# Weights cast in a software DMA, first loads in pieces and cast on VectorE, and one set of transposes moved by a batch: attention followed by a gated feed-forward, on one core

## The chip, the cores and the metric

The kernel runs on one core of one Trainium2 chip. The metric is the device time of one execution in microseconds (us); lower is better. Medians are over all executions of a kernel; ratios use only those in the fast state. The profile's span is about 1.8 us shorter than the time of the same execution. Two executions in this study (of some 55 of the changed kernels) were far slower than all others; they are shown below, and no ratio uses them.

Names: TensorE is PE, VectorE is DVE, ScalarE is ACT, GpSimd is POOL, SyncE is SP in the profile's lines. PEld is TensorE's weight load. `L203` is line 203 of that kernel's file, so the same operation has different line numbers in different kernels.

## The reference

Eight batches. Grouped attention (16 query heads, 4 key heads, 384 positions, 64 per head), whose output is the input of a feed-forward with a gate that mixes positions:

```python
scores = softmax(q @ k.T / sqrt(D));  x = scores @ v          # per batch and head
h = relu(x @ w_in)                    # 1024 -> 1024
u, v = h[..., :512], h[..., 512:]
v_n = (v - mean(v)) / sqrt(var(v) + 1e-6)
v_s = einsum('ts,bsd->btd', w_spatial, v_n) + b_spatial
out = (u * v_s) @ w_out               # 512 -> 1024
```

All inputs and the output are float32; the kernel computes in float16 with float32 sums.

## The kernel before

TensorE's program order is written by hand. Batch `b`'s attention is nine visits of two score tiles each; into the visits are put the matmuls that sum the values, the transposes of the next batch's k and q, and, from the third visit on, the feed-forward of the batch before (`pv`: the v half of w_in, `pu`: the u half, `psp`: w_spatial, `po`: w_out). So no feed-forward runs during batch 0: there, TensorE has little to do, and until the first `pv` of batch 0's feed-forward (in batch 1's third visit) everything hangs on loads, casts and ScalarE's exp.

The weights are staged: a load on SyncE's queue into one of three float32 buffers, then a cast to float16 on VectorE.

```python
stage = ctx.enter_context(tc.tile_pool(name="stage", bufs=3))
...
def load_w_in(kc):                       # eight of these, four loads each
    st_w = stage.tile([P, DFF], FP32, name=f"st_wi_{kc}", tag="st_w")
    ...
            nc.sync.dma_start(st_w[32 * i : 32 * (i + 1), :], moe_w_in[r0 : r0 + 32, :])
    nc.vector.tensor_copy(w_in16[:, kc, :], st_w)

def load_w_out(m):                       # four of these
    st_w = stage.tile([P, DM], FP32, name=f"st_wo_{m}", tag="st_w")
    nc.sync.dma_start(st_w, moe_w_out[m * P : (m + 1) * P, :])
    nc.vector.tensor_copy(w_out16[:, m, :], st_w)
...
def load_batch(b):
    load_kv(b); load_q(b, 0); load_v(b); load_q(b, 1)      # all on SyncE's queue
    cast_kv(b); cast_q(b, 0); cast_v(b); cast_q(b, 1)      # all on GpSimd
...
load_batch(0)
load_consts()
with tc.manual_schedule(engines={PE}):
    transpose_k(0)
    transpose_q(0, 0, 0); transpose_q(0, 0, 1)
    transpose_q(0, 1, 0); transpose_q(0, 1, 1)             # second group pair, ahead of all scores
    load_bias()
    for kc in range(NKT):
        load_w_in(kc)
    load_ws()                                              # w_spatial
    for m in range(NDT):
        load_w_out(m)
    for b in range(B + 1):
        for vi in range(VISITS if b < B else 1):
            scores(b, [2 * vi, 2 * vi + 1])
            ...
            if vi == 1 and b + 1 < B:
                load_batch(b + 1)
            if b + 1 < B and vi in (4, 5, 6, 7, 8):        # next batch's k, then all its q
                if vi == 4: transpose_k(b + 1)
                else:       transpose_q(b + 1, (vi - 5) // 2, (vi - 5) % 2)
            if b == 0 and vi in (3, 4, 5):
                transpose_ws(vi - 3)
            if vi == 2 and b > 0 or b == B:
                queue += feed_forward(b - 1)
            ...
```

(Lines joined and cut.) The loads of batch 1 come behind all the weights in SyncE's queue, and its first load waits for nothing else.

The softmax here doesn't subtract the row's maximum and nothing guards it: scores larger than these inputs give would overflow.

## Time and profile before

| | before |
|---|---|
| time, median of 3 | 327.24 us |
| profile's span | 324.8 us |
| TensorE busy over the span | 83% |
| first `pv` of batch 0 starts | 65.2 us |
| TensorE busy before that / after that | 26.2 of 65.2 us / 244.2 of 259.6 us |

The table of busy time by stretch, before (columns: stretch in us, then busy us and number of instructions of PE, PEld, DVE, ACT, POOL, then granted TensorE clock, DMA share, GB/s):

```profile
0.00:65.20 65.20, 26.17 (x261) 11.84 (x261) 22.88 (x46) 26.25 (x32) 15.96 (x25) 0.81 0.84 239
65.20:324.80 259.60, 244.20 (x2198) 113.43 (x2196) 139.06 (x270) 159.92 (x218) 23.43 (x29) 0.99 0.26 89
```

From the first `pv` on TensorE is busy 94% of the time, so waits can cost at most 6% there. Before it, TensorE, VectorE, ScalarE and GpSimd are all idle more than half of the time: waits rule. The page's rows of busy tenths, in 40 slices of 8.1 us, before:

```profile
PE   1470118799998999899989998999989998999994
PEclk9996558989999999999999999999999999999999
```

The zero-to-one slices at 24 to 49 us are the hole. What TensorE waited for there, before (who waited for what: us in total, times, longest):

```profile
PE psw_352 L203 <- DVE ws_240 L194: 15.1, 3, 14.6
PE pk_366 L214 <- POOL k_1_281 L111: 6.8, 1, 6.8
PE pk_141 L214 <- POOL k_0_118 L111: 5.0, 1, 5.0
PE pq_1_0_168 L229 <- POOL q_0_1_125 L125: 3.6, 1, 3.6
```

`psw` is a transpose of w_spatial: it waited for VectorE's cast of w_spatial. `pk_366` is the transpose of k_1: it waited for GpSimd's cast of k_1. Neither cast was late for want of an engine: both engines stood idle until the load landed. The chain of waits, before, cut to this stretch (start us, us, what), shows what stood behind them:

```profile
32.15 0.42 SPq L181
32.57 0.04 issue
32.61 0.42 SPq L181
33.03 0.04 issue
33.08 5.17 DMA ws_238<-in_moe_w_spatial_dram
38.24 0.02 issue
38.27 1.80 DVE ws_240 L194 x3
40.07 0.05 issue
40.11 0.30 PE psw_352 L203
```

`SPq L181` is SyncE issuing loads of w_in: w_spatial was loaded only at 33 us, when the last of w_in had found a staging buffer. The same queue makes k_1 later still; GpSimd's timeline, before:

```profile
47.23 0.83 POOL L111 CAST k_1_281<-k_1_273 128x768 f16<-128x768 f32 x1 [33.71 <-DMA k_1_273<-in_k_dram]
```

GpSimd sat idle 33.71 us for a load that was issued behind w_out.

SyncE's queue stopped from 18.0 to 25.75 us in the middle of w_in. VectorE's timeline, before:

```profile
24.10 0.56 DVE L288 TENSOR_TENSOR xt_307<-X_0_0_0_324,rec_0_0_321 128x384 f16<-128x384 f32 x1 [7.87 <-ACT rec_0_0_321 L284]
25.04 0.68 DVE L182 CAST w_in_107<-st_wi_196 128x1024 f16<-128x1024 f32 x1
```

The cast that frees the buffer stands behind batch 0's x (`xt`) in VectorE's order, and VectorE was idle 7.87 us until x could be computed.

### The profile page before, as it was taken

The numbers are of one execution on the slowest core, as the hardware profiler recorded it, in microseconds if no ns is written. First come the engines' busy times: TensorE is split into PE (matmuls) and PEld (weight loads), VectorE is DVE, ScalarE is ACT, GpSimd is POOL, SyncE is SP. The second block draws the span as 40 slices with busy tenths as digits, with TensorE's granted clock in tenths as the row PEclk, the third lists the DMA queues.
The fourth block names the chain that finished last, engine by engine and source line by source line (L and its number), as shares of the span: only waits on it lengthen the run. The fifth ranks groups of instructions, "written<-read, shape, count | busy, mean of one in ns | idle before, by whom it ended". The sixth has DMA issues, their size and how long they took to land.

```text
span 324.8 us, 5856 instructions
## 1 busy us (share of the span) xinstructions
PE 270.4 (83%) x2457; PEld 125.3 (39%) x2457; DVE 161.9 (50%) x316; ACT 186.2 (57%) x249; POOL 39.4 (12%) x54
## 2 busy tenths in 40 slices
PE   1470118799998999899989998999989998999994
PEld 0320003344443544345434543354435443443451
DVE  1604434326653655365645384366546553654574
ACT  1090027946667755857585748576667568675300
POOL 3300015541111111101120112000000000000000
PEclk9996558989999999999999999999999999999999
DMA  7927989994256016601560002100310031003104
GB/s 242 240 68 171 316 262 300 315 302 123 56 196 207 0 50 226 211 1 50 194 218 30 0 23 108 67 0 2 132 65 2 1 131 65 2 0 131 67 0 194
DMA packets 30828, 38.71 MB, mean 119 GB/s; under 512 B 1489, under 2 KB 26066, under 8 KB 30802
## 3 DMA queue, kind: packets, MB, share of 16 engines
q1 hardware_dynamic: 30802, 38.35, 37.0%
q8 instruction: 19, 0.31, 0.4%
q14 instruction: 7, 0.06, 0.1%
HBM read 25.76 MB, written 12.58 MB: 118 GB/s over the span
## 4 chain that ended last, share of the span: by engine, by line
PE 65%; ACT 19%; DMA 7%; SPq 3%; DVE 2%; issue 1%; POOL 1%; DVEq 0%
DMA q_0_1_116<-in_q_dram 3%; DMA q_1_0_275<-in_q_dram 2%; ACT aT_0_262 L257 2%; SPq L181 2%; DMA ws_238<-in_moe_w_spatial_dram 2%; ACT aT_1_3573 L257 1%; ACT aT_1_2647 L257 1%; ACT aT_1_759 L257 1%; ACT aT_1_3119 L257 1%; ACT aT_1_2175 L257 1%; ACT aT_1_1703 L257 1%; ACT aT_1_1231 L257 1%; ACT aT_1_364 L257 1%; PE pv_0_627 L303 1%; ACT aT_0_545 L257 1%
## 5 line engine op out<-in xcount | busy, mean ns | idle before, releaser
L340 PEld LDWEIGHTS <-w_in_107 128*128 128x128 f16 x256 | 24.1, 98 | 18.2 <-issue 2.6
L272 PEld LDWEIGHTS <-ones_103 128*32 128x32 f16 x384 | 7.4, 97 | 15.8 <-issue 14.1
L203 PE MATMUL psw_352<-ident_102,ws_240 128*128 128x128 f16 x3 | 0.9, 287 | 15.1 <-DVE ws_240 L194 15.1
L257 ACT ACTIVATE aT_0_262<-sc_8_357 128x1024 f16<-128x1024 f32 x1 | 1.0, 1024 | 16.9 <-PE sc_8_357 L244 16.9
L257 ACT ACTIVATE aT_0_262<-sc_0_256 128x1024 f16<-128x1024 f32 x1 | 1.0, 1024 | 13.6 <-PE sc_0_256 L244 13.6
L203 PEld LDWEIGHTS <-ws_240 128*128 128x128 f16 x9 | 0.9, 117 | 15.9 <-DVE ws_240 L194 15.9
L214 PE MATMUL pk_366<-ident_102,k_1_281 128*128 128x128 f16 x6 | 0.8, 310 | 6.8 <-POOL k_1_281 L111 6.8
L257 ACT ACTIVATE aT_1_364<-sc_10_380 128x1024 f16<-128x1024 f32 x1 | 1.0, 1024 | 6.9 <-PE sc_10_380 L244 6.9
L214 PE MATMUL pk_141<-ident_102,k_0_118 128*128 128x128 f16 x6 | 0.8, 310 | 5.0 <-POOL k_0_118 L111 5.0
L244 PEld LDWEIGHTS <-kT_148 64*128 64x128 f16 x36 | 1.8, 102 | 8.3 <-issue 7.9
L111 POOL CAST k_1_281<-k_1_273 128x768 f16<-128x768 f32 x1 | 0.8, 829 | 33.7 <-DMA k_1_273<-in_k_dram 33.7
L288 DVE TENSOR_TENSOR xt_307<-X_0_0_0_324,rec_0_0_321 128x384 f16<-128x384 f32 x1 | 0.6, 557 | 7.9 <-ACT rec_0_0_321 L284 7.9
L303 PEld LDWEIGHTS <-xt_307 128*128 128x128 f16 x24 | 2.6, 113 | 4.1 <-issue 2.3
L356 PEld LDWEIGHTS <-bias_ones 128*128 128x128 f16 x32 | 3.1, 98 | 1.9 <-issue 0.7
L229 PE MATMUL pq_1_0_168<-ident_102,q_0_1_125 128*128 128x128 f16 x6 | 0.8, 307 | 3.6 <-POOL q_0_1_125 L125 3.6
L272 PEld LDWEIGHTS <-v_0_123 128*32 128x32 f16 x96 | 2.9, 109 | 2.0 <-issue 1.0
L214 PEld LDWEIGHTS <-k_1_281 128*128 128x128 f16 x6 | 0.6, 137 | 7.7 <-POOL k_1_281 L111 7.7
L379 PEld LDWEIGHTS <-gT_3919 128*128 128x128 f16 x24 | 2.3, 98 | 3.0 <-DVE gT_3919 L365 0.5
L303 PEld LDWEIGHTS <-xt_3511 128*128 128x128 f16 x24 | 2.3, 98 | 2.9 <-issue 0.3
L379 PEld LDWEIGHTS <-gT_2267 128*128 128x128 f16 x24 | 2.2, 97 | 3.0 <-DVE gT_2267 L365 0.6
L379 PEld LDWEIGHTS <-gT_2739 128*128 128x128 f16 x24 | 2.2, 97 | 3.0 <-DVE gT_2739 L365 0.6
L379 PEld LDWEIGHTS <-gT_3211 128*128 128x128 f16 x24 | 2.2, 97 | 3.0 <-DVE gT_3211 L365 0.6
(1178 smaller groups left out, 812.1 us busy)
## 6 DMA issues: line engine op xcount, KB each, us to landing
q_0_0_112<-in_q_dram SPq DMA_DIRECT2D x1, 768.0 KB, 5.6
q_0_1_116<-in_q_dram SPq DMA_DIRECT2D x1, 768.0 KB, 9.4
q_1_0_275<-in_q_dram SPq DMA_DIRECT2D x1, 768.0 KB, 7.6
q_1_1_279<-in_q_dram SPq DMA_DIRECT2D x1, 768.0 KB, 9.5
q_2_0_602<-in_q_dram SPq DMA_DIRECT2D x1, 768.0 KB, 5.5
q_2_1_606<-in_q_dram SPq DMA_DIRECT2D x1, 768.0 KB, 5.5
q_3_0_1074<-in_q_dram SPq DMA_DIRECT2D x1, 768.0 KB, 6.2
q_3_1_1078<-in_q_dram SPq DMA_DIRECT2D x1, 768.0 KB, 6.2
```

The costliest lines, as they stand in the source:

```text
L111: nc.gpsimd.tensor_copy(k16, loaded[("k32", b)].rearrange("p g (t d) -> p t g d", t=NST))
L181: nc.sync.dma_start(st_w[32 * i : 32 * (i + 1), :], moe_w_in[r0 : r0 + 32, :])
L203: nc.tensor.transpose(psw[:, tt, :], ws16[:, tt, st, :], ident16)
L214: nc.tensor.transpose(pk[:, gp, t, :], k16[:, t, 2 * gp : 2 * gp + 2, :].rearrange("p g d -> p (g d)"), ident16,)
L229: nc.tensor.transpose(pq[:, jj, t, :], q16[:, t, 2 * jp + jj, :, :].rearrange("p h d -> p (h d)"), ident16,)
L244: nc.tensor.matmul(sc[:, half, :], kT[b][lo:hi, gp, t, :], rhs[lo:hi, c * 512 : (c + 1) * 512], start=True, stop=True,)
L257: nc.scalar.activation(aT[b, gp][:, t, :, c * 512 : (c + 1) * 512], sc, AF.Exp, scale=scale)
L272: nc.tensor.matmul(dst[32 * i : 32 * (i + 1), 0:S], weights(t, half), a[:, t, half, j * S : (j + 1) * S], start=(t == 0), stop=(t == NST - 1),
L303: nc.tensor.matmul(pv, xt[:, kc, st * P : (st + 1) * P], w_in16[:, kc, DH:DFF], start=(kc == 0), stop=(kc == NKT - 1),)
L340: nc.tensor.matmul(pu[:, 0:S], w_in16[:, kc, mu * P : (mu + 1) * P], xT[b][:, kc, :], start=(kc == 0), stop=(kc == NKT - 1),)
L356: nc.tensor.matmul(psp[:, 0:S], bias_ones, bias_rows, start=True, stop=False)
L379: nc.tensor.matmul(po, gT[:, m, tt * P : (tt + 1) * P], w_out16[:, m, half * 512 : (half + 1) * 512], start=(m == 0), stop=(m == NDT - 1),)
```

## The change

Its intent: no staging of weights, an earlier first score, and transposes only when they are needed. The diff, cut to its core:

```diff
-    stage = ctx.enter_context(tc.tile_pool(name="stage", bufs=3))
+    stage = ctx.enter_context(tc.tile_pool(name="stage", bufs=1))
...
-    def load_w_in(kc):            # 4 loads on nc.sync into st_w, cast by nc.vector
+    def load_w_in(c0, c1):        # 16 casting DMAs for the columns c0:c1
+        for gp in range(2):
+            for half in range(2):
+                for quad in range(2):
+                    ...
+                    for jq in range(2):
+                        i = half * 2 + jq
+                        nc.gpsimd.dma_start(
+                            w_in16[32 * i : 32 * (i + 1), kc : kc + 2, c0:c1], rows[jq]
+                        )
-    def load_w_out(m):            # likewise staged
+    def load_w_out():
+        for h in range(2):
+            nc.gpsimd.dma_start(w_out16[:, 2 * h : 2 * h + 2, :], ...)
...
-    load_batch(0)
     load_consts()
-    with tc.manual_schedule(engines={PE}):
+    with tc.manual_schedule(engines={PE, POOL, SP}):
+        load_k(0)
+        load_q(0, 0, pieces=2)
+        cast_k(0, nc.vector)
+        cast_q(0, 0, nc.vector)
+        load_v(0)
+        load_q(0, 1, pieces=2)
+        cast_v(0, nc.gpsimd)
+        cast_q(0, 1, nc.gpsimd)
+        load_w_in(DH, DFF)        # v half first
+        load_w_in(0, DH)
+        load_w_out()
         transpose_k(0)
         transpose_q(0, 0, 0)
         transpose_q(0, 0, 1)
-        transpose_q(0, 1, 0)
-        transpose_q(0, 1, 1)
...
-                    if vi == 1 and b + 1 < B:
-                        load_batch(b + 1)
-                    if b + 1 < B and vi in (4, 5, 6, 7, 8):
+                    if vi in (1, 2):
+                        transpose_q(b, 1, vi - 1)          # second pair inside its own batch
+                    if vi == 2 and b + 1 < B:
+                        load_batch(b + 1, nc.vector if b == 0 else nc.gpsimd)
+                    if vi >= 6 and b + 1 < B:              # next batch: k and first pair only
...
-                    if b == 0 and vi in (3, 4, 5):
-                        transpose_ws(vi - 3)
+                    if b == 0 and vi == 3:
+                        load_ws()
+                        load_bias()
...
+                    if b == 1:
+                        queue[7:7] = [(0.2, lambda st=st: transpose_ws(st)) for st in range(NST)]
```

`cast_k` and `cast_q` for batch 1 run on VectorE, for later batches on GpSimd; `cast_v` and the second pair's `cast_q` always on GpSimd. A load that changes the type must be issued from GpSimd (the Trainium skill, "DMA: Bandwidth & Descriptors", SWDGE vs HWDGE vs iDMA), so the weights change queue as well as caster.

More of the change, by code (lines that the diff above doesn't have):

```diff
@@ L14 @@
 ALU = mybir.AluOpType
-PE = mybir.EngineType.PE
+PE, POOL, SP = mybir.EngineType.PE, mybir.EngineType.Pool, mybir.EngineType.SP
 @with_exitstack
@@ L89, with load_k @@
     loaded = {}
-    def load_kv(b):
+    def load_k(b):
         k32 = ld.tile([P, HKV, NST * D], FP32, name=f"k32_{b}", tag="k32")
         nc.sync.dma_start(k32, k[b].rearrange("g (p t) d -> p g (t d)", t=NST))
-        loaded[("k32", b)] = k32
+        loaded["k32", b] = k32
     def load_v(b):
@@ L98, in load_v, with load_q, cast_k, cast_v @@
         nc.sync.dma_start(v32, v[b].rearrange("g (p t) d -> p g (t d)", t=NST))
-        loaded[("v32", b)] = v32
-    def load_q(b, gp):
+        loaded["v32", b] = v32
+    def load_q(b, gp, pieces=1):
         q32 = ld.tile([P, 2 * G, NST * D], FP32, name=f"q32_{b}_{gp}", tag=f"q32_{gp}")
-        nc.sync.dma_start(
-            q32,
-            q[b, gp * 2 * G : (gp + 1) * 2 * G].rearrange("h (p t) d -> p h (t d)", t=NST),
-        )
-        loaded[("q32", b, gp)] = q32
-    def cast_kv(b):
-        k16 = qk16.tile([P, NST, HKV, D], FP16, name=f"k16_{b}", tag="k16")
-        nc.gpsimd.tensor_copy(
-            k16, loaded[("k32", b)].rearrange("p g (t d) -> p t g d", t=NST)
-        )
-        loaded[("k16", b)] = k16
-    def cast_v(b):
+        n = 2 * G // pieces
+        for i in range(pieces):
+            h0 = gp * 2 * G + i * n
+            nc.sync.dma_start(
+                q32[:, i * n : (i + 1) * n, :],
+                q[b, h0 : h0 + n].rearrange("h (p t) d -> p h (t d)", t=NST),
+            )
+        loaded["q32", b, gp] = q32
+    def cast_k(b, engine):
+        k16 = qk16.tile([P, NST, HKV, D], FP16, name=f"k16_{b}", tag="k16")
+        engine.tensor_copy(k16, loaded["k32", b].rearrange("p g (t d) -> p t g d", t=NST))
+        loaded["k16", b] = k16
+    def cast_v(b, engine):
         v16 = qk16.tile([P, HKV, NST, D], FP16, name=f"v16_{b}", tag="v16", bufs=3)
-        nc.gpsimd.tensor_copy(v16.rearrange("p g t d -> p g (t d)"), loaded[("v32", b)])
-        loaded[("v16", b)] = v16
-    def cast_q(b, gp):
+        engine.tensor_copy(v16.rearrange("p g t d -> p g (t d)"), loaded["v32", b])
+        loaded["v16", b] = v16
+    def cast_q(b, gp, engine):
         q16 = qk16.tile([P, NST, G, 2, D], FP16, name=f"q16_{b}_{gp}", tag=f"q16_{gp}")
-        q32 = loaded[("q32", b, gp)]
+        q32 = loaded["q32", b, gp]
         for half in range(2):
-            nc.gpsimd.tensor_copy(
+            engine.tensor_copy(
                 q16[:, :, :, half, :],
@@ L128, in cast_q, with load_batch @@
             )
-        loaded[("q16", b, gp)] = q16
-    def load_batch(b):
-        load_kv(b)
+        loaded["q16", b, gp] = q16
+    def load_batch(b, first):
+        load_k(b)
         load_q(b, 0)
+        cast_k(b, first)
+        cast_q(b, 0, first)
         load_v(b)
         load_q(b, 1)
-        cast_kv(b)
-        cast_q(b, 0)
-        cast_v(b)
-        cast_q(b, 1)
+        cast_v(b, nc.gpsimd)
+        cast_q(b, 1, nc.gpsimd)
     ident = cst.tile([P, P], FP32, name="ident")
@@ L171, in load_bias @@
         nc.vector.tensor_copy(lo, lo32)
-    def load_w_in(kc):
-        gp, quad, jj = kc // 4, (kc // 2) % 2, kc % 2
-        st_w = stage.tile([P, DFF], FP32, name=f"st_wi_{kc}", tag="st_w")
-        for half in range(2):
-            for jq in range(2):
-                i = half * 2 + jq
-                head = gp * 2 * G + half * G + quad * 2 + jq
-                r0 = head * D + 32 * jj
-                nc.sync.dma_start(st_w[32 * i : 32 * (i + 1), :], moe_w_in[r0 : r0 + 32, :])
-        nc.vector.tensor_copy(w_in16[:, kc, :], st_w)
-    def load_w_out(m):
-        st_w = stage.tile([P, DM], FP32, name=f"st_wo_{m}", tag="st_w")
-        nc.sync.dma_start(st_w, moe_w_out[m * P : (m + 1) * P, :])
-        nc.vector.tensor_copy(w_out16[:, m, :], st_w)
+    def load_w_in(c0, c1):
+        for gp in range(2):
+            for half in range(2):
+                for quad in range(2):
+                    r0 = (gp * 2 * G + half * G + 2 * quad) * D
+                    rows = moe_w_in[r0 : r0 + 2 * D, c0:c1].rearrange(
+                        "(jq jj r) n -> jq r jj n", jq=2, jj=2
+                    )
+                    kc = gp * 4 + quad * 2
+                    for jq in range(2):
+                        i = half * 2 + jq
+                        nc.gpsimd.dma_start(
+                            w_in16[32 * i : 32 * (i + 1), kc : kc + 2, c0:c1], rows[jq]
+                        )
+    def load_w_out():
+        for h in range(2):
+            nc.gpsimd.dma_start(
+                w_out16[:, 2 * h : 2 * h + 2, :],
+                moe_w_out[2 * h * P : (2 * h + 2) * P, :].rearrange("(m p) n -> p m n", p=P),
+            )
     def load_ws():
@@ L417 @@
         transpose_q(0, 0, 1)
-        transpose_q(0, 1, 0)
-        transpose_q(0, 1, 1)
-        load_bias()
-        for kc in range(NKT):
-            load_w_in(kc)
-        load_ws()
-        for m in range(NDT):
-            load_w_out(m)
         total = sum(t for t, _ in feed_forward(0))
@@ L439 @@
                 if b < B:
-                    if vi == 1 and b + 1 < B:
-                        load_batch(b + 1)
-                    if b + 1 < B and vi in (4, 5, 6, 7, 8):
-                        if vi == 4:
+                    if vi in (1, 2):
+                        transpose_q(b, 1, vi - 1)
+                        done += T_TRANS
+                    if vi == 2 and b + 1 < B:
+                        load_batch(b + 1, nc.vector if b == 0 else nc.gpsimd)
+                    if vi >= 6 and b + 1 < B:
+                        if vi == 6:
                             transpose_k(b + 1)
                         else:
-                            transpose_q(b + 1, (vi - 5) // 2, (vi - 5) % 2)
+                            transpose_q(b + 1, 0, vi - 7)
                         done += T_TRANS
-                    if b == 0 and vi in (3, 4, 5):
-                        transpose_ws(vi - 3)
-                if vi == 0 and b > 0:
-                    pass
+                    if b == 0 and vi == 3:
+                        load_ws()
+                        load_bias()
                 if vi == 2 and b > 0 or b == B:
                     queue += feed_forward(b - 1)
+                    if b == 1:
+                        queue[7:7] = [(0.2, lambda st=st: transpose_ws(st)) for st in range(NST)]
                 if b == 0:
```

## The prediction

> **What bounds the kernel now.** Two regimes. From 65.3 us to the end (324.8 us) TensorE is busy 244.1 of 259.5 us (table of busy time by stretch): that stage is TensorE-bound. Before 65.3 us TensorE is busy only 26.3 us. The loss is in batch 0, before batch 0's feed-forward starts (first pv matmul at 65.2 us, timeline). The waits show where: first scores at 15.0 us, after loads and casts on GpSimd (last of them, q second pair, landed 11.8 us, cast 1.7 us); 14.6 us waiting for the w_spatial cast, which lies behind the eight w_in stagings (16 transfers' queue, SyncE waiting for staging buffers); 6.8 us for the k_1 cast, whose load is issued behind w_out (GpSimd waits 33.7 us for it). ScalarE, at 0.91 us per exp, is idle 16.9 and 6.9 us there. TensorE's clock is granted at 0.57 from 25 to 40 us.
>
> **What the change does.** It removes 12 staged loads and 12 VectorE casts of 0.69 us (8.3 us, not themselves the limit), and with them the queue that blocks w_spatial and batch 1. Batch 1's k, q, v can then load at 5 to 20 us. First scores need only k and q's first pair, cast on VectorE in about 0.5 us each (from the 0.69 us of a 128x1024 cast) instead of 0.82: first exp at about 9.7 us instead of 15.6. Batch 0's attention is then 18 exps of 0.91 plus three 1.05 us reciprocals, so batch 1 could begin near 30 us (59.5 before) and feed-forward near 36 us. If nothing else limited, the gain would be near 28 us.
>
> **What it adds.** 34 DMAs on GpSimd's in-order queue, after the casts of v_0 and q's second pair (about 12.6 us). Behind them, in the same queue (the built instruction order shows it), are the casts of v_1 (0.83) and q_1 second pair (1.60), and TensorE needs that q in batch 1's second visit, before any feed-forward. No software DMA is in the trace. The Trainium skill ("DMA: Bandwidth & Descriptors", Specifications) gives about 1 us first-byte latency for this path; taking 1 us as the queue's cost per DMA (estimate): 12.6 + 34 + some for the larger w_out ones + 2.4 = about 50 us, feed-forward at about 51 us instead of 65.2. At 0.6 us each it would be about 38 us. Transfer alone: 6.3 MB of weights plus about 4 MB of batches 1 and 2 and w_spatial, at the measured 300 GB/s, 34 us, end near 47 us; the last of that (w_out) is not needed early. Fewer casts run on VectorE while GpSimd writes descriptors, so I expect little of the port lock ("SBUF — State Buffer", Who interferes with whom), 1 to 3 us.
>
> The moved transposes add no work; w_spatial's transposes (about 1 us) now come after feed-forward starts. Steady state unchanged.
>
> **Prediction.** Mostly GpSimd-limited, between those cases: 311 us, range 299 to 322. Faster by over 2%: 0.82; within 2%: 0.13; slower: 0.05.
>
> **What would show it.** First exp near 10 us; first pv matmul at 42 to 54 us, and the wait ahead of it on GpSimd's cast of q_1's second pair, with GpSimd filled by DMA issue before it; from first pv to the end about 260 us, as before; clock at 0.5 for a shorter time.
>
> **What would make it wrong.** Software DMA at over 1.4 us each (gain gone) or below 0.5 us (then under 300, limited by transfer or exps); casting transfers much slower than 300 GB/s, so that pv waits for w_in; w_spatial's cast, early in VectorE's order, holding batch 0's x.

## The result, and the profile after

The changed kernel took 302.5 us (median of 4; 301.24 to 303.34) beside 326.34 us for the kernel before in the same rounds. The ratio is 0.9266 (95% interval 0.9211 to 0.9322). Ratios here and below are the mean time of one kernel's fast runs over that of the other's in the same rounds, so not quite the ratio of the medians quoted. The control, in the experiments below, gave 302.11 us and 0.9275.

| | before | after |
|---|---|---|
| span | 324.8 | 301.4 |
| first exp | 15.6 | 12.3 |
| first `pv` starts | 65.2 | 41.2 |
| first `pu` starts | 71.8 | 47.7 |
| from first `pu` to the end | 253.0 | 253.7 |

All of the gain lies ahead of the first `pu`. I use its start as the measure below, rather than that of `pv`, because the 24 `pv` matmuls themselves take longer where the clock is still low (6.5 us after, 5.2 us in `e_both` below, where it was full). TensorE's timeline at that point, before and after:

```profile
71.82 1.46 PE L340 MATMUL pu_0_679<-xt_307,w_in_107 128*128 128x384 f16 x8
47.71 1.46 PE L348 MATMUL pu_0_640<-xt_271,w_in_107 128*128 128x384 f16 x8
```

Busy time by stretch, after:

```profile
0.00:41.20 41.20, 23.14 (x252) 11.36 (x253) 18.70 (x36) 26.57 (x33) 26.15 (x49) 0.91 1.00 228
41.20:301.40 260.20, 246.04 (x2208) 114.06 (x2205) 143.00 (x274) 157.75 (x217) 27.07 (x34) 0.99 0.30 101
```

The second stretch is as long as before (260.2 and 259.6 us). Busy tenths in 40 slices of 7.5 us, after; the hole is gone:

```profile
PE   0576879899899989999899989999899989999993
PEclk9977979999999999999999999999999999999998
```

TensorE's waits, after; the waits of 15.1 and 6.8 us are no longer there:

```profile
PE pk_177 L222 <- DVE ident_102 L155: 9.6, 1, 9.6
PE X_0_1_1_375 L280 <- DVE xt_271 L296: 2.5, 1, 2.5
PE pq_1_0_545 L237 <- POOL q_1_1_260 L126: 1.2, 1, 1.2
```

The second line is what is left of the w_spatial wait. VectorE's order has w_spatial's cast ahead of batch 0's x, and the load of w_spatial landed at 23.5 us (10.2 us after its issue, against 5.2 before; the DMA share was 1.12 from 12 to 24 us), so x waited and the matmul that needs its buffer waited for x. The third line is the wait for the cast of q_1's second pair, which stands behind all the weights in GpSimd's queue. GpSimd's timeline, after, from 12.8 us (start us, us, what, count, and in brackets the idle time before it):

```profile
12.82 4.38 POOL L186 DMA_DIRECT2D w_in_107<-in_moe_w_in_dram  x8
19.22 1.08 POOL L186 DMA_DIRECT2D w_in_107<-in_moe_w_in_dram  x2 [2.01 <-DMA w_in_107<-in_moe_w_in_dram]
...
28.90 6.31 POOL L186 DMA_DIRECT2D w_in_107<-in_moe_w_in_dram  x12 [1.05 <-DMA w_in_107<-in_moe_w_in_dram]
35.19 1.47 POOL L192 DMA_DIRECT2D w_out_108<-in_moe_w_out_dram  x2
36.62 0.87 POOL L119 CAST v_1_258<-v_1_254 128x768 f16<-128x768 f32 x1
37.39 1.63 POOL L126 CAST q_1_1_260<-q_1_1_256 128x768 f16<-128x768 f32 x2
```

One w_in DMA occupies GpSimd for 0.54 us; eight are in flight at most (the next waits for the completion of the one eight before), which adds 5.3 us of waiting to 18.6 us of issue. The cast that TensorE waits for ends at 39.0 us.

The start, on VectorE's timeline, after:

```profile
4.16 0.95 DVE L114 CAST k_0_128<-k_0_123 128x768 f16<-128x768 f32 x1 [2.48 <-DMA k_0_123<-in_k_dram]
5.31 0.95 DVE L126 CAST q_0_0_130<-q_0_0_125 128x768 f16<-128x768 f32 x1 [0.20 <-DMA q_0_0_125<-in_q_dram]
8.45 0.95 DVE L126 CAST q_0_0_130<-q_0_0_125 128x768 f16<-128x768 f32 x1 [2.19 <-DMA q_0_0_125<-in_q_dram]
9.32 0.22 DVE L155 CAST ident_102<-ident 128x128 f16<-128x128 f32 x1
```

The second piece of q came only at 8.45 us (the whole of it was cast from 6.87 us on before), one cast takes 0.95 us on VectorE against 0.80 to 0.83 on GpSimd, and the identity's cast, which every transpose needs, has got behind them. TensorE therefore starts at 9.6 us, though k_0 was ready at 5.1.

### The profile page after: what moved, and what is told of

Same layout as the page of the kernel before. It is cut to its first block, busy times and chain, and to the rows that moved or that the text cites. A ratio compares the mean times of both kernels' runs of the same rounds, so it can differ in the third digit from the quotient of the medians.

```text
span 301.4 us, 5836 instructions
## 1 busy us (share of the span) xinstructions
PE 269.2 (89%) x2457; PEld 125.4 (42%) x2457; DVE 161.7 (54%) x310; ACT 184.3 (61%) x249; POOL 53.2 (18%) x82
## 4 chain that ended last, share of the span: by engine, by line
PE 69%; ACT 16%; DMA 6%; DVE 4%; issue 2%; SPq 1%; POOL 0%; DVEq 0%
DMA ws_316<-in_moe_w_spatial_dram 3%; DMA q_0_1_135<-in_q_dram 3%; ACT aT_1_720 L265 1%; ACT aT_0_2385 L265 1%; ACT aT_0_969 L265 1%; ACT aT_1_335 L265 1%; ACT aT_0_1441 L265 1%; ACT aT_0_489 L265 1%; PE pv_0_588 L311 1%; ACT aT_0_3329 L265 1%; ACT aT_0_1913 L265 1%; ACT aT_0_2857 L265 1%; ACT aT_1_2613 L265 1%; ACT aT_1_3539 L265 1%; ACT aT_1_3085 L265 1%
## 5 line engine op out<-in xcount | busy, mean ns | idle before, releaser
L348 PEld LDWEIGHTS <-w_in_107 128*128 128x128 f16 x256 | 23.9, 98 | 21.6 <-issue 6.9
L186 POOL DMA_DIRECT2D w_in_107<-in_moe_w_in_dram x32 | 17.1, 543 | 5.3 <-DMA w_in_107<-in_moe_w_in_dram 5.3
L280 PEld LDWEIGHTS <-ones_103 128*32 128x32 f16 x384 | 7.4, 96 | 15.1 <-issue 13.3
L222 PE MATMUL pk_177<-ident_102,k_0_128 128*128 128x128 f16 x6 | 0.8, 303 | 9.6 <-DVE ident_102 L155 9.6
L265 ACT ACTIVATE aT_0_209<-sc_0_203 128x1024 f16<-128x1024 f32 x1 | 1.0, 1024 | 10.3 <-PE sc_0_203 L252 10.3
L114 POOL CAST k_3_1060<-k_3_1056 128x768 f16<-128x768 f32 x1 | 0.8, 827 | 33.0 <-DVE stats_0_1086 L321 33.0
L114 POOL CAST k_6_2476<-k_6_2472 128x768 f16<-128x768 f32 x1 | 0.8, 827 | 27.7 <-DMA k_6_2472<-in_k_dram 27.7
L114 POOL CAST k_5_2004<-k_5_2000 128x768 f16<-128x768 f32 x1 | 0.8, 827 | 26.6 <-DMA k_5_2000<-in_k_dram 26.6
L114 POOL CAST k_7_2948<-k_7_2944 128x768 f16<-128x768 f32 x1 | 0.8, 827 | 25.4 <-DMA k_7_2944<-in_k_dram 25.4
L114 POOL CAST k_4_1532<-k_4_1528 128x768 f16<-128x768 f32 x1 | 0.8, 827 | 25.1 <-DMA k_4_1528<-in_k_dram 25.1
L202 DVE CAST ws_318<-ws_316 128x384 f16<-128x384 f32 x3 | 1.9, 671 | 5.2 <-DMA ws_316<-in_moe_w_spatial_dram 5.2
L222 PEld LDWEIGHTS <-k_0_128 128*128 128x128 f16 x6 | 0.6, 133 | 9.5 <-DVE k_0_128 L114 5.2
L311 PEld LDWEIGHTS <-xt_271 128*128 128x128 f16 x24 | 2.7, 116 | 3.5 <-issue 1.6
L387 PEld LDWEIGHTS <-gT_3623 128*128 128x128 f16 x24 | 2.2, 98 | 3.5 <-issue 0.7
L387 PEld LDWEIGHTS <-gT_3895 128*128 128x128 f16 x24 | 2.3, 98 | 3.0 <-DVE gT_3895 L373 0.5
L387 PEld LDWEIGHTS <-gT_2697 128*128 128x128 f16 x24 | 2.2, 97 | 3.0 <-DVE gT_2697 L373 0.6
L387 PEld LDWEIGHTS <-gT_1753 128*128 128x128 f16 x24 | 2.2, 97 | 3.0 <-DVE gT_1753 L373 0.6
L387 PEld LDWEIGHTS <-gT_2225 128*128 128x128 f16 x24 | 2.2, 97 | 3.0 <-DVE gT_2225 L373 0.6
L387 PEld LDWEIGHTS <-gT_1281 128*128 128x128 f16 x24 | 2.2, 97 | 3.0 <-DVE gT_1281 L373 0.6
```

Of the source, the lines that this page charges most:

```text
L114: engine.tensor_copy(k16, loaded["k32", b].rearrange("p g (t d) -> p t g d", t=NST))
L186: nc.gpsimd.dma_start(w_in16[32 * i : 32 * (i + 1), kc : kc + 2, c0:c1], rows[jq])
L202: nc.vector.tensor_copy(ws16[:, tt, :, :], ws32[:, tt, :].rearrange("p (s t) -> p t s", t=NST))
L222: nc.tensor.transpose(pk[:, gp, t, :], k16[:, t, 2 * gp : 2 * gp + 2, :].rearrange("p g d -> p (g d)"), ident16,)
L265: nc.scalar.activation(aT[b, gp][:, t, :, c * 512 : (c + 1) * 512], sc, AF.Exp, scale=scale)
L280: nc.tensor.matmul(dst[32 * i : 32 * (i + 1), 0:S], weights(t, half), a[:, t, half, j * S : (j + 1) * S], start=(t == 0), stop=(t == NST - 1),
```

## The experiments

Two theories. **A, queue order**: the gain comes from taking the weights out of the in-order queue in which w_spatial and batch 1 wait; who casts them matters little. And what bounds the start now is two gates in parallel, GpSimd's queue and w_spatial's cast, both opening near 39 us. **B, cast relief**: what counts is that the casting DMA does away with staging and with 8.3 us of VectorE's casts, and that scores start earlier. Times are medians, ratios are to the kernel before in the same rounds. All twelve results were correct.

| kernel | time | ratio (95%) | first `pu` | span |
|---|---|---|---|---|
| after | 302.5 | 0.9266 (0.9211 to 0.9322) | 47.7 | 301.4 |
| `after_again` (control) | 302.11 | 0.9275 (0.9247 to 0.9304) | 46.9 | 299.7 |
| `e_order` | 310.91 | 0.9541 (0.9497 to 0.9585) | 55.4 | 308.4 |
| `e_order_gp` | 301.5 (fast runs 301.09) | 0.9239 (0.9182 to 0.9297) | slow profile | |
| `e_order_gp2` (the same) | 302.3 | 0.9271 (0.9251 to 0.9291) | 47.8 | 300.8 |
| `e_staged` | 320.79 | 0.9847 (0.9779 to 0.9915) | 65.7 | 319.3 |
| `e_trans_back` | 312.94 | 0.96 (0.9552 to 0.9647) | 56.5 | 311.3 |
| `e_first_old` | 302.18 | 0.9284 (0.923 to 0.9337) | 47.1 | 300.2 |
| `e_ws_pool` | 302.67 | 0.9282 (0.9246 to 0.9317) | 47.5 | 300.8 |
| `e_pool_first` | 305.25 (fast runs 305.1) | 0.9331 (0.9274 to 0.9387) | slow profile | |
| `e_pool_first2` (the same) | 302.67 | 0.929 (0.9266 to 0.9313) | 47.3 | 301.0 |
| `e_both` | 299.09 | 0.9163 (0.9103 to 0.9223) | 41.2 | 294.7 |
| `e_best` | 296.94 | 0.9111 (0.9076 to 0.9146) | 40.7 | 294.2 |

In every profile in the fast state, before and after included, the span is the start of the first `pu` plus 252.8 to 254.9 us. So one number per profile, the time at which batch 0's feed-forward gets going, tells the result.

### Order alone, on the kernel before: `e_order`

```diff
-    with tc.manual_schedule(engines={PE}):
+    with tc.manual_schedule(engines={PE, SP}):
         load_bias()
+        load_ws()
+        load_batch(1)
         for kc in range(NKT):
             load_w_in(kc)
-        load_ws()
...
-                    if vi == 1 and b + 1 < B:
+                    if vi == 1 and 0 < b and b + 1 < B:
```

> The kernel before, with one edit: the loads of w_spatial and of batch 1 are issued on the SyncE queue ahead of the weights (staging, VectorE casts, transposes and first casts unchanged). Theory A (queue order): the gain comes from the weights no longer standing ahead of w_spatial and batch 1 in an in-order queue; who casts them matters little. Then the first pv matmul starts at 42 to 47 us instead of 65.2, the two long waits of TensorE (14.6 and 6.8 us) vanish, and the span is about 303 to 308 us. Theory B (the software casting DMA and its relief of staging and of VectorE's 8.3 us are what count): staging through three buffers goes on setting when the weights are there, the first pv matmul waits for them until 55 us or later, and the span is above 314 us.

The first `pv` starts at 40.8 us, as early as in the changed kernel, and both long waits are gone. But it does not run through. TensorE's waits in `e_order`:

```profile
PE pv L303 <- DVE w_in L182: 5.6, 3, 2.0
```

So the first `pu` starts at 55.4 us, the time is 310.91 us and the span 308.4: as A said, the two long waits vanished; A's span (303 to 308) was missed by 0.4 us, and B's (above 314) by 5.6. Order alone gives 15 of the 24 us. The rest is w_in arriving late. Two causes could do that: VectorE reaching its staging casts late, since they stand in its order behind batch 0's x, or three buffers and the transfer.

### Order, and the staging casts on GpSimd: `e_order_gp`, `e_order_gp2`

`e_order` plus:

```diff
-        nc.vector.tensor_copy(w_in16[:, kc, :], st_w)
+        nc.gpsimd.tensor_copy(w_in16[:, kc, :], st_w)
-        nc.vector.tensor_copy(w_out16[:, m, :], st_w)
+        nc.gpsimd.tensor_copy(w_out16[:, m, :], st_w)
```

> e_order (the kernel before with w_spatial and batch 1 loaded ahead of the weights) plus the weights' 12 staging casts moved from VectorE to GpSimd. In e_order the first pv started at 40.8 us but waited 5.6 us for w_in, because the staging buffers were held until VectorE reached its casts, which stand in its order behind batch 0's x. If that order of VectorE is the rest of the difference to the kernel after, the wait for w_in vanishes or falls below 2 us, pu starts at 48 to 50 us instead of 55.4, and the span is 301 to 304 us: the casting DMA as such is then not needed. If the three staging buffers and the transfer are the limit, the wait for w_in stays at 4 us or more and the span above 306.

> e_order_gp unchanged, since its only profile fell into an execution in which every matmul took twice as long. In a normal execution: first pv at 40 to 42 us with under 2 us of waiting for w_in, pu near 48 us, time 300 to 302, within 0.7% of after_again: no casting DMA and no moved transposes, only queue order and casts on an idle engine.

The first run's profile fell in an execution of 675.22 us, see below; its other three took 300.44 to 301.91 us. The second run was normal: 302.3 us, and no wait for w_in at all. Its first `pv` and `pu` stand at 40.9 and 47.8 us, those of the changed kernel at 41.2 and 47.7. In the same rounds its ratio is 0.9271, that of the changed kernel 0.9275.

So the whole gain is to be had without a casting DMA, without pieces and without moving a transpose: the loads in another order on the same queue, and twelve casts on an engine that had nothing to do. Moving the casts was worth 8.6 us (310.91 to 302.3, on different chips). GpSimd takes longer for one (1.04 us against 0.68), so it was not their length but their place. In `e_order` VectorE cast the first three pieces between batch 0's x, while they held all three staging buffers; in `e_order_gp2` GpSimd cast them as they landed. The two timelines, `e_order` (VectorE) and then `e_order_gp2` (GpSimd):

```profile
25.41 0.68 DVE L182 CAST w_in<-st_wi 128x1024 f16<-128x1024 f32 x1
32.28 0.68 DVE L182 CAST w_in<-st_wi 128x1024 f16<-128x1024 f32 x1
38.93 0.68 DVE L182 CAST w_in<-st_wi 128x1024 f16<-128x1024 f32 x1
21.41 1.04 POOL L182 CAST w_in<-st_wi 128x1024 f16<-128x1024 f32 x1 [0.63 <-DMA st_wi<-in_moe_w_in_dram]
23.55 1.04 POOL L182 CAST w_in<-st_wi 128x1024 f16<-128x1024 f32 x1 [1.10 <-DMA st_wi<-in_moe_w_in_dram]
25.73 1.04 POOL L182 CAST w_in<-st_wi 128x1024 f16<-128x1024 f32 x1 [1.14 <-DMA st_wi<-in_moe_w_in_dram]
```

That part of B is right, and A's "who casts them matters little" is wrong: what VectorE has to do for the weights counts.

One kernel was not run: the casts on GpSimd with the loads in their old order. SyncE's stop of 7.7 us in the kernel before hangs on VectorE's cast too, so the casts alone may gain there. The 15 and the 8.6 us are shares in this sequence of edits; how the gain divides otherwise is not shown.

### The software DMA alone undone: `e_staged`

The changed kernel with the old `load_w_in` and `load_w_out` (three staging buffers, SyncE, VectorE), called in the same place; everything else as changed.

> The kernel after with the software DMA alone undone: weights staged by SyncE and cast on VectorE, ahead of batch 1 as in the kernel before; first loads, first casts and moved transposes as in the kernel after. Queue-order theory: most of the gain is gone, since k_1 is again behind w_out; TensorE waits for k_1's cast until 45 to 50 us, first pv at 55 to 62 us, span 314 to 322. If instead the early start and the moved transposes carried the gain, the span would stay below 308.

320.79 us: of the 24 us, 5 are left (a gain of 1.5%, under the 2% of a verdict, so "unclear"). TensorE waits again for what stands behind the weights:

```profile
PE pk L215 <- DVE k L114: 20.8, 1, 20.8
```

k_1's load was issued at 37.9 us, behind w_out. The early scores and the moved transposes are worth little where the queue is blocked. This is A's first half from the other side; VectorE's staging casts, again behind batch 0's x, slow the same queue here, so this run does not part the two.

### The transposes alone undone: `e_trans_back`

```diff
-                    if vi in (1, 2):
+                    if b == 0 and vi in (1, 2):
                         transpose_q(b, 1, vi - 1)
...
-                    if vi >= 6 and b + 1 < B:
-                        if vi == 6:
+                    if vi >= 4 and b + 1 < B:
+                        if vi == 4:
                             transpose_k(b + 1)
                         else:
-                            transpose_q(b + 1, 0, vi - 7)
+                            transpose_q(b + 1, (vi - 5) // 2, (vi - 5) % 2)
```

> The kernel after with the second pair of batches 1 to 7 transposed in the batch before again (batch 0's own stay in batch 0). TensorE then meets the transposes of q_1's second pair inside batch 0's last visits, and their cast stands behind 34 DMAs on GpSimd until 39 us: the wait for it grows from 1.2 to 4 to 8 us, first pv at 46 to 49 us instead of 41.2, span 306 to 309. If the move of the transposes were neutral, span within 1 us of 301.4.

312.94 us, 10.8 more than the control; the span is 311.3 us, where I had expected 306 to 309. TensorE's waits:

```profile
PE pq L237 <- POOL q L126: 5.7, 1, 5.7
PE X L280 <- DVE xt L296: 3.7, 1, 3.7
```

The wait for GpSimd grows to 5.7 us as expected. It costs more than its own length because it now comes before batch 0's last two score tiles, so all of that, and batch 1's first three visits, come after 39.6 us; in the changed kernel they were done while GpSimd's queue drained. The move of the transposes adds no work and saves none; it makes the software DMA bearable, by letting TensorE meet its queue one batch later.

### The first loads and casts alone undone: `e_first_old`

```diff
-        load_q(0, 0, pieces=2)
-        cast_k(0, nc.vector)
-        cast_q(0, 0, nc.vector)
+        load_q(0, 0)
+        cast_k(0, nc.gpsimd)
+        cast_q(0, 0, nc.gpsimd)
...
-        load_q(0, 1, pieces=2)
+        load_q(0, 1)
```

> The kernel after with whole first loads of q (no pieces) and the casts of k_0 and q_0's first pair back on GpSimd. If the pieces and VectorE's casts made the early start, first exp moves from 12.3 towards 15 us and the span grows by 2 us. If the early start comes from no longer transposing the second pair ahead of the first scores, first exp stays at 11 to 12.5 us, and the span within 1 us of the kernel after (301.4), as the gates near 39 us hide it anyway.

The first exp comes at 10.4 us, 1.9 us earlier than with pieces and VectorE, and the time is that of the control. That part of the change does harm to the start, and the harm is hidden: TensorE's wait for GpSimd's cast of q_1's second pair grows from 1.2 to 3.7 us, and the first `pu` still starts at 47.1 us. What made the first exp earlier than 15.6 us is that the second pair's transposes no longer stand ahead of the scores.

### The two gates: `e_ws_pool`, `e_pool_first`, `e_both`

`e_ws_pool` moves the casts of w_spatial and of the bias off VectorE:

```diff
-            nc.vector.tensor_copy(
+            nc.gpsimd.tensor_copy(
                 ws16[:, tt, :, :], ...
-        nc.vector.tensor_copy(hi, b_tp)        # and the two bias lines after it
+        nc.gpsimd.tensor_copy(hi, b_tp)
```

> The kernel after, with the casts of w_spatial and of the bias moved from VectorE to GpSimd's queue (behind the cast of q_1's second pair). The 2.46 us wait of TensorE for x (held behind the w_spatial cast in VectorE's order) goes to 0. Theory A (two gates in parallel, GpSimd's queue and w_spatial's cast, both ending near 39 us): the wait for the cast of q_1's second pair grows from 1.2 to about 3.5 us and the first pv matmul stays within 0.7 us of 41.2; span unchanged, about 301. Rival (the wait for w_spatial was a plain loss in series): first pv at about 38.8, span 2.4 us less.

`e_pool_first` (and `e_pool_first2`, the same) puts batch 1's casts ahead of half of the weights on GpSimd:

```diff
         load_w_in(DH, DFF)
-        load_w_in(0, DH)
-        load_w_out()
...
                     if vi == 2 and b + 1 < B:
                         load_batch(b + 1, nc.vector if b == 0 else nc.gpsimd)
+                        if b == 0:
+                            load_w_in(0, DH)
+                            load_w_out()
```

> The kernel after, with batch 1's casts of v and of q's second pair put ahead of the second half of w_in and of w_out in GpSimd's queue. Cast of q_1's second pair ends near 29 us instead of 39. Theory A: the 1.21 us wait before pq_1_0 goes to 0, the w_spatial wait of 2.46 us stays; first pv matmul at about 40 us, span about 1.2 us less than after (300). If GpSimd was the only gate, first pv would be at about 37.5 us. If the weights come too late now, pv or pu waits for w_in.

> e_pool_first unchanged, since its only profile fell into a slow execution (granted clock 0.66). In a normal execution, by the parallel gates: no wait for the cast of q_1's second pair, but the wait for x behind w_spatial's cast of 2 to 5 us stays, first pv at 39 to 41 us, time within 1% of after_again.

`e_both` has both edits.

> Both edits together. Theory A (parallel gates): more than the sum of the two alone: about 3.7 us less than after, first pv matmul at 37 to 38 us, span 297 to 298, with no wait over 1 us in TensorE between first scores and first pv apart from those for exp. Rival (series): the sum of the two single gains. If the transfer of the weights is the limit beneath, pv or pu waits for w_in and the gain stays below 2 us.

With w_spatial out of the way the wait just moves. TensorE's waits in `e_ws_pool`:

```profile
PE pq L237 <- POOL q L126: 5.6, 1, 5.6
```

That is 4.4 us more than after, for 2.5 us taken away (the first exp also came 0.9 us earlier there), and the first `pu` stands at 47.5 us: no gain. With GpSimd's order changed instead, the other wait stays. In `e_pool_first2`:

```profile
PE X L280 <- DVE xt L296: 2.8, 1, 2.8
```

Again no gain (302.67 us, 47.3 us); I had expected one of 1.2 us in this case, and in the repeat the first `pv` at 39 to 41 us, where it came at 42.1. Two things stand in the way of the 1.2 us: in its place TensorE waits 1.0 and 0.5 us for ScalarE's exps, and the granted clock was 0.50 to 0.84 from 27 to 36 us in this profile. With both edits neither wait is there. TensorE's waits in `e_both` up to 50 us, all that the view lists (the first is the start):

```profile
PE pk L222 <- DVE ident L155: 8.1, 1, 8.1
PE sc L252 <- ACT aT L265: 6.2, 10, 1.2
```

The time is 299.09 us, and the first `pu` starts at 41.2 us. The ratio fell from 0.9282 and 0.9331 to 0.9163 in the same rounds. This is the mark of two gates in parallel: each alone is worth nothing, both are worth about 3.5 us in the median.

The profiles differ by more, 6.5 us at the first `pu`, and not all of it is the gates'. Part is the start: in the profiled run q's second piece was cast from 6.98 us and the first exp came at 10.9 us, against 8.45 and 12.3 after, and with the gates gone such a difference of 1.5 us is no longer hidden. Part is the clock: it was full in every 3 us up to 48 us in `e_both`, but 0.67 to 0.76 from 15 to 21 us, 0.50 from 27 to 30 and 0.69 to 0.74 from 39 to 45 us after, and the `pv` matmuls took 5.2 us instead of 6.5. What is left, from the first exp to the first `pv`, is 25.1 us against 28.9, a difference of 3.8: about the two waits of 2.5 and 1.2 us, with a share of the clock in it that no run separates.

The four executions of `e_both` spread over 296.48 to 300.77 us, and the profiled one was the fastest. The others have no trace, but the record gives their clocks: 0.998 for the fastest, 0.988 for the slowest (though 1.0 for one of 298.31 us). In `e_best` below, the three executions at 0.996 to 0.998 took 295.35 to 295.98 us, the three at 0.991 and 0.992 took 297.9 to 298.64. So spread and clock go together in part; what sets the clock was not tested.

### All of it: `e_best`, with `after_again` as the control

`e_both` plus the edit of `e_first_old`.

> The kernel after, unchanged, as a control on the same chip as the three others: about 302 us; its first pv matmul at 41 to 42 us again.

> e_both (batch 1's casts ahead of half of the weights on GpSimd, casts of w_spatial and bias on GpSimd) with whole first loads and first casts on GpSimd as in e_first_old, which had its first exp at 10.4 us instead of 12.3. With both gates gone the early start is no longer hidden: first exp near 10.4, first pv near 35.5 to 36.5 us, time 296 to 299, that is 3 to 6 us less than after_again. If the start stays hidden by something else, no better than e_both's 299.

The control repeated the result; its w_spatial wait was 3.2 us and its GpSimd wait 0.4, so the two gates stand close enough for their order to change from run to run. `e_best` took 296.94 us (295.35 to 298.64) beside 302.11 us. The intervals of their ratios, 0.9076 to 0.9146 and 0.9247 to 0.9304, do not meet. It beats both kernels. TensorE's waits in `e_best` up to 50 us, all that the view lists:

```profile
PE sc L252 <- ACT aT L265: 6.4, 10, 1.2
PE pk L222 <- POOL k L114: 5.1, 1, 5.1
PE pq L237 <- POOL q L126: 2.4, 1, 2.4
```

The last two end before the first exp, at 8.2 us; from there on TensorE waits for nothing but ScalarE's exp. Moving the first exp from 10.9 (`e_both`) to 10.4 us gave 0.5 us at the first `pu`: no longer hidden.

### Two slow executions

One execution of `e_pool_first` took 399.14 us and one of `e_order_gp` 675.22 us. Both were the profiled ones. The `pv` matmuls of the two (columns: count, then ns min/median/max, first and last start):

```profile
L311 PE MATMUL pv<-w_in,xt x192: 451/524/525, 43.2 to 372.7; 128*128 128x512 f16 x192
L303 PE MATMUL pv<-w_in,xt x192: 688/785/921, 52.9 to 632.4; 128*128 128x512 f16 x192
```

A normal one has a median of 379 ns. Every `pv` matmul was slower throughout (451 and 688 ns at the least), while busy time on ScalarE stayed at 184.6 and 190.1 us (184.3 after). The first has a recorded clock of 0.659; the second has 1.0, though its `pv` matmuls took twice as long. The same kernels, run again, showed nothing of the kind in four executions each, so nothing ties it to the edits. Its cause stays open.

## Why the prediction was right, and where a step was off

- **What bounds the kernel, and where the gain lies: right.** The stretch after the first `pv` was predicted at about 260 us and measured 260.2. The two long waits vanished.
- **Cost of a software DMA: the term mis-sized.** The prediction took 1 us for each of the 34 from the Trainium skill's figure for this path ("DMA: Bandwidth & Descriptors", Specifications), and called it an estimate. The trace shows 0.54 us of GpSimd for a w_in DMA and 0.75 for a w_out one, 18.6 us in all, and 5.3 us of waiting for completions, which the prediction left out. That sums to 24 us, where the prediction had 34 and some more for w_out. First `pv` came at 41.2 us, just outside the 42 to 54 us given, and so the time, 302.5 us, in the lower part of the range. The 311 us lay between two cases of cost per DMA, and the trace is near the cheaper one (0.6 us, feed-forward at about 38 us). That 299 to 322 us held it owes something to the width of the range.
- **Start of the scores: wrong in three terms.** 9.7 us was predicted, 12.3 measured. VectorE's casts of k and q took 0.95 us each, not about 0.5: I had scaled a contiguous 128x1024 cast (0.69 us) to one that permutes its axes. The second piece of q landed at 8.45 us, 1.6 us later than the whole had. And the identity's cast got behind both, which the built order showed and I passed over. None of it reached the time (`e_first_old`).
- **"The moved transposes add no work": true and misleading.** Nothing was costed for them, yet without the move the kernel takes 10.8 us longer.
- **w_spatial's cast in VectorE's order** was named only as a risk. It is a gate of the same height as GpSimd's queue: taking GpSimd's away alone gained nothing. So "mostly GpSimd-limited" did not hold: GpSimd's cast of q_1 was the last wait of more than 1 us before the first `pv`, as forecast, but it held TensorE for only 1.2 us, not until 51.
- **"8.3 us, not themselves the limit"** of VectorE's casts was right of their length and missed their place. In the kernel before, SyncE already stood 7.7 us for a buffer that one of these casts had to free. With the order of the loads mended they become the limit (`e_order` against `e_order_gp2`), through the buffers they hold.
- **The port lock** of 1 to 3 us ("SBUF — State Buffer", Who interferes with whom) was not seen: the 32 w_in DMAs took 532 to 673 ns, with a median of 534.
- **The clock** was lower for a shorter time, as predicted: 0.81 on average over the 65.2 us before the first `pv`, 0.91 over 41.2 us now.

The largest error of judgement is one that the forecast of the time did not bring out: I took the casting DMA for the means, where the order of SyncE's loads and the place of twelve casts in VectorE's order were the cause.

## What to carry to other kernels

Where a load is late, look first at what stands ahead of it in its in-order queue; giving the urgent loads their turn and the casts to an idle engine gained here as much as a new kind of DMA with a new schedule around it. A queue that is relieved hands its burden to another one: list what stands behind the moved work there, too, and move its consumers accordingly. When a wait is taken away and nothing happens, look for a second gate at the same height before calling it free: here each of two edits gained nothing, and both together gained about 3.5 us in the median.

## What the Trainium skill lacked or had wrong

- "DMA: Bandwidth & Descriptors", Specifications: about 1 us first-byte latency for a DMA from GpSimd is not what one costs its queue. GpSimd was busy 0.54 us with one of 32 partitions by two rows of 2 KB, and 0.75 us with one of 128 partitions by two rows of 4 KB (float32 read, float16 written). The page has no such figure by shape.
- I found nothing on that page on how many of these a kernel keeps in flight. In this kernel as built the ninth waits for the first, and with other loads in flight, a median of 5.4 us from issue to landing made that 5.3 us of waiting in 32.
- "VectorE: DVE Perf Modes", Mode 2×_2P: two float32 results a cycle in SBUF if the outermost dimensions of source and destination are both even, or equal. The contiguous cast took 0.69 us for 1024 elements a partition, the permuting one (three by four by 64) 0.95 us for 768, which is 0.67 and 1.24 ns per element. As the program writes it, the second has an outermost size of three on both sides, so by that rule it could keep the mode, yet it took nearly twice as long per element. Whether it lost the mode, or its strides cost the time, no run here takes apart.
- "TensorE: Matmul & The Clock Gate", Seeing it yourself, warns that recorded clock events can be unreliable. A run here agrees: a recorded clock of 1.0 beside `pv` matmuls of 785 ns, against 379 ns in a normal run. The page mentions a clock stuck low for 50 us and more, but no state of half the speed for a whole execution of 673.5 us, nor one of 524 ns at a recorded 0.659.
- I found no page with a figure for what splitting a load does to the landing of its last piece. Of q's first pair in two pieces the second was cast from 8.45 us on in the changed kernel (6.98 to 9.02 in the other runs with pieces), whole from 6.58 to 6.87 us (profiles in the fast state).
